# Decode attention and MLP on one core: K and V in tiles of four heads instead of two

## The chip, the cores and the metric

The kernel runs on one core of a Trainium2 chip. The metric is the device time of one execution in microseconds (us). Engines: PE (matrix products, with weight loads shown as PEld), DVE (vector), ACT (scalar), POOL, and SP, which here only issues DMAs. 16 DMA engines move data between HBM and SBUF.

## The reference, cut to what matters

One token, x of 576 numbers, goes through an attention block over a cached window and through an MLP; a gate mixes the two.

```python
W = 4096; Hq, Hkv, Dh = 32, 16, 128; D = 576; F = 4608
q = (x @ wq).reshape(1, 1, 32, 128)
k = repeat(k_cache[:, :, Sk - W:, :], 2); v = repeat(v_cache[:, :, Sk - W:, :], 2)   # Sk = 32768
p = softmax(einsum(q, k) * Dh ** -0.5)
a = einsum(p, v).reshape(1, 1, 4096) @ wo
b = gelu_tanh(x @ w1 + b1) @ w2 + b2
g = sigmoid(sum(x * gate_w))
out = g * a + (1 - g) * b
```

All tensors are bf16. K and V windows are 16.8 MB each, wq and wo 4.7 MB each, w1 and w2 5.3 MB each: 53.6 MB that are read once.

## The kernel before

All large loads are issued by SP, in program order. A K or V tile holds two heads: partition p holds 64 positions of one head, 16 KB (`load_kv`, L99). Six such buffers are used in turn by K, V and at the end w2 (`kv_pool`); three buffers hold wq, then w1, then wo (`w_pool`). A load into a buffer waits until its last reader is done, and what stands behind it in SP's queue waits with it.

The work is cut into 16 units (`NU`, half a tile each). For each unit h, `transposes` (L243) turns the keys with 32 matmuls against an identity, in eight groups of four; each group of 512 columns is copied out of PSUM, three by DVE (L257), five by ACT (L259). `scores` (L271) then multiplies q with the turned keys, two groups of four matmuls a unit. q lies in `qz` between zeros, so that each matmul puts its rows where they belong and adds zeros to the others. With two heads to a tile, turned keys of both heads alternate in the columns; a mask takes away those of the other head.

Four units make a batch of 128 rows by 512 columns. `softmax` (L287) runs in four steps: `row_max` (mask and maximum, DVE), `turn_max` (the maximum over rows, through PE), `spread` (the exponential on ACT), `put` (four PE transposes and eight DVE copies into `ez`, the form in which the weights stand for the next product). There are four batches. `values` (L346) multiplies ez with V, eight matmuls a unit, summed in `acc`; `heads_out` (L363) takes the heads from acc (four DVE operations on `a_s`) and turns them by one matmul.

The loop at L562 writes the order by hand: in loop h stand the transposes of unit h + 1, the scores of unit h, one step of the waiting softmax (`chain`), of heads_out (`tail`) or of the gelu (`mlp`), and the values of unit h - 6. w1's two halves are multiplied (`w1_mul`, 36 matmuls each) after loops 2 and 8; then `gelu` turns the 4608 numbers of h by 36 matmuls of 64 columns (L494). After the loop come the last softmax, the last values, wo's product (L684, 64 matmuls), w2's first three quarters in the same PSUM tile, `part_s` (L692), the last quarter of w2 into `y_ps` (L703), and the output.

Of the kernel before, what the change touches and what calls it, by code (L numbers as in the profile page):

```python
# [16 lines left out]
def kernel(  # L17
# [24 lines left out]
    NCK = W // (P // 2)  # L42
    NCH = NCK // 2
    NU = 2 * (Hkv // 2)
# [19 lines left out]
    HB = 4  # L64
    NB = Hkv // HB
    R = 2 * HB
    RP = R // 2
    BC = 4
    NBL = NCH // BC
    NGR = 2 * NBL // NQ  # L70
    MASK = -1.0e30


# [3 lines left out]
    kv_pool = ctx.enter_context(tc.tile_pool(name="kv_pool", bufs=6))  # L77
    w_pool = ctx.enter_context(tc.tile_pool(name="w_pool", bufs=3))
    const = ctx.enter_context(tc.tile_pool(name="const", bufs=1))
    kT_pool = ctx.enter_context(tc.tile_pool(name="kT_pool", bufs=2))  # L80
    small = ctx.enter_context(tc.tile_pool(name="small", bufs=2))
# [13 lines left out]
    OJ = 8  # L95
# [3 lines left out]
    def load_kv(cache, m, name):  # L99
        t = kv_pool.tile([P, NCK, Dh], BF16, name=name, tag="kv")  # L100

        nc.sync.dma_start(
            out=t[:],
            in_=cache[0, 2 * m : 2 * m + 2, Sk - W : Sk, :].rearrange(
                "e (p c) d -> p e (c d)", c=NCK
            ),
        )
        return t
# [46 lines left out]
    k_tiles[1] = load_k(1)  # L155

# [5 lines left out]
    qz = const.tile([P, Hkv // 2, 56], BF16, name="qz")  # L162
# [17 lines left out]
    for o in range(2):  # L180
# [22 lines left out]
    row_e = const.tile([P, 2], FP32, name="row_e")  # L203
    nc.vector.tensor_reduce(
        out=row_e[:], in_=ident_f[:].rearrange("p (a e q) -> p e a q", e=2, q=2), axis=AX.XY,
        op=ALU.add,
    )
    nc.vector.tensor_scalar(
        out=row_e[:], in0=row_e[:], scalar1=-MASK, scalar2=MASK, op0=ALU.mult, op1=ALU.add
    )  # L210
    mask = const.tile([P, BC * P], BF16, name="mask")
    for e in range(2):
        nc.vector.tensor_copy(
            out=mask[:, e::2], in_=row_e[:, e : e + 1].to_broadcast([P, BC * P // 2])
        )
# [15 lines left out]
    nc.gpsimd.memset(x2[:], 0.0)  # L231

# [10 lines left out]
    def transposes(h, i):  # L243
# [3 lines left out]
        for c in range(BC):  # L247
            nc.tensor.matmul(  # L248
                tp[:, c * P : (c + 1) * P],
                lhsT=k_tiles[h // 2][:, (h % 2) * NCH + i * BC + c, :],  # L250
                rhs=ident[:],
                start=True,
                stop=True,
            )
# [9 lines left out]

    ez = const.tile([P, 2, HB // 2, 2 * NBL, BC, R], BF16, name="ez")
    nc.gpsimd.memset(ez[:].rearrange("p a b c d e -> p (a b c d e)"), 0.0)
    b1_r = const.tile([P, 2, FB], BF16, name="b1_r")
    nc.gpsimd.memset(b1_r[:], 0.0)
    sums = const.tile([P, NB], FP32, name="sums")

    def scores(h, s):  # L271

        b, ul = h // HB, h % HB
        if ul == 0 and s == 0:
            s_tiles[b] = ps_s.tile([P, BC * P], FP32, name="s_ps", tag="s")
        lo = R * (NGR - 1 - 2 * (h % 2) - s)
        for t in range(NQ):
            i = 4 * s + t
            nc.tensor.matmul(  # L279
                s_tiles[b][32 * t : 32 * (t + 1), :],  # L280
                lhsT=qz[:, h // 2, lo : lo + 32],
                rhs=kT[h][:, i * BC * P : (i + 1) * BC * P],
                start=(ul == 0 and s == 0),
                stop=(ul == HB - 1 and s == 1),
            )

    def softmax(b):  # L287
# [3 lines left out]
        ms = small.tile([P, BC * P], FP32, name="ms", tag="ms")  # L291
        m8 = small.tile([1, R], FP32, name="m8", tag="m8")
        m_all = small.tile([1, P], FP32, name="m_all", tag="m_all")
        nb = small.tile([P, 1], FP32, name="nb", tag="nb")
        pr = small.tile([P, BC * P], BF16, name="pr", tag="pr")

        def row_max():
            nc.vector.tensor_tensor_reduce(
                out=ms[:], in0=s_ps[:], in1=mask[:], scale=1.0, scalar=-3.0e38,
                op0=ALU.add, op1=ALU.max, accum_out=mx[:],  # L300
            )

        def turn_max():
# [3 lines left out]
                out=m8[:], in_=mT[:].rearrange("o (s r) -> o r s", r=R), axis=AX.X, op=ALU.max  # L307
            )
            nc.vector.tensor_copy(
                out=m_all[:].rearrange("o (s r) -> o s r", r=R),  # L310
                in_=m8[:].rearrange("o (s r) -> o s r", s=1).to_broadcast([1, P // R, R]),
            )

        def spread():
# [6 lines left out]
                out=pr[:], in_=ms[:], func=ACT.Exp, bias=nb[:, 0:1], scale=SCALE,  # L321
                accum_out=sums[:, b : b + 1],
            )

        def put():
            pT = ps_m.tile([P, BC, P], BF16, name="pT", tag="m")
            for c in range(BC):
                nc.tensor.transpose(  # L328
                    out=pT[:, c, :], in_=pr[:, c * P : (c + 1) * P], identity=ident[:]
                )  # L330
            for m in range(HB // 2):
                for s in range(NGR):
                    nc.vector.tensor_copy(  # L333
                        out=ez[:, b % 2, m, NQ * s : NQ * (s + 1), :, RP * m : RP * (m + 1)],
                        in_=pT[:].rearrange("p c (t s r) -> p t c s r", t=NQ, r=R)[
                            :, :, :, s, RP * m : RP * (m + 1)
                        ],
                    )

        return [row_max, turn_max, spread, put]  # L340
# [5 lines left out]
    def values(h, i):  # L346

        b, ul = h // HB, h % HB
        if ul == 0 and i == 0:

            pool, tag = (ps_t, "tp") if b == NB - 1 else (ps_o, "o")
            acc[b] = pool.tile([P, BC, Dh], FP32, name="acc", tag=tag)
        ct = i % NQ
        n = (h % 2) * NBL + i
        nc.tensor.matmul(  # L355
            acc[b][32 * ct : 32 * ct + 4 * R, :, :],
            lhsT=ez[:, b % 2, ul // 2, n, :, :].rearrange("p c r -> p (c r)"),
            rhs=v_tiles[h // 2][:, n * BC : (n + 1) * BC, :],
            start=(ul == 0 and i < NQ),
            stop=(ul == HB - 1 and i >= NBL - NQ),  # L360
        )

    def heads_out(b):  # L363


        def take():
            nc.vector.tensor_scalar(
                out=a_s[:], in0=acc[b][:, 0, :], scalar1=m_c[:, 0:1], scalar2=None, op0=ALU.mult
            )
            for c in range(1, BC):  # L370
                nc.vector.scalar_tensor_tensor(  # L371
                    out=a_s[:], in0=acc[b][:, c, :], scalar=m_c[:, c : c + 1], in1=a_s[:],
# [3 lines left out]
        def turn_out():  # L376
            o_ps = ps_m.tile([P, R], FP32, name="o_ps", tag="m")
            nc.tensor.matmul(o_ps[:], lhsT=a_s[:], rhs=m_r[:], start=True, stop=True)  # L378
            nc.vector.tensor_copy(out=o_sb[:, b * R : (b + 1) * R], in_=o_ps[:])
# [34 lines left out]
    for h in range(2):  # L414
        for i in range(NBL):
            transposes(h, i)

# [14 lines left out]
    qT = ps_m.tile([P, QC // Dh, 2, NB], FP32, name="qT", tag="m")  # L432
# [10 lines left out]
    for m in range(HB // 2):  # L443
        lo = R * (NGR - 1) + RP * m
        nc.vector.tensor_copy(  # L445
            out=qz[:, m :: HB // 2, lo : lo + RP],
            in_=qT[:, :, m, :].rearrange("p i b -> p b i"),
# [29 lines left out]
    def gelu():  # L477
# [3 lines left out]
        h_r = const.tile([P, 2, FB], FP32, name="h_r")  # L481
        box = []

        def take():
            nc.vector.tensor_tensor(  # L485
                out=h_r[:], in0=h_box[0][:, :, 0:FB], in1=b1_r[:], op=ALU.add
            )
            box.append(ps_m.tile([P, RJ, NG], FP32, name="hT", tag="m"))

        def turn_h(j):  # L490

            rows = h_r[:].rearrange("p k n -> p (k n)")
            for e in range(2):
                nc.tensor.matmul(  # L494
                    box[0][64 * e : 64 * (e + 1), j, :],
                    lhsT=rows[:, j : j + RJ * 63 + 1 : RJ],
                    rhs=sel_f[:, e, :],
                    start=True,
                    stop=True,
                )  # L500

        def act():
            hacc = const.tile([P, NF], FP32, name="hacc")
            nc.vector.tensor_copy(out=hacc[:], in_=box[0][:].rearrange("p j g -> p (j g)"))
# [23 lines left out]
    def norm():  # L528

        sg = const.tile([P, NB, R], FP32, name="sg")  # L530
        nc.vector.tensor_tensor(
            out=sg[:],
            in0=sums[:].rearrange("p (b o) -> p b o", o=1).to_broadcast([P, NB, R]),
            in1=m_r[:].rearrange("p (o r) -> p o r", o=1).to_broadcast([P, NB, R]),
# [23 lines left out]
    W1_AT = {1: 0, 7: 1}  # L558
    LAG = HB + 2
    chain, tail, mlp = [], [], []  # L560
    w1_ready = None
    for h in range(NU):  # L562
        if 1 <= h < NU - 3 and h % 2 == 1:
            k_tiles[(h + 3) // 2] = load_k((h + 3) // 2)
        if h >= HB and h % 2 == 0:
            v_tiles[(h - HB) // 2] = load_v((h - HB) // 2)
        if h == 1:

            for o in range(2):
                nc.sync.dma_start(  # L570
                    out=b1_r[o : o + 32 * (NQ - 1) + 1 : 32],
                    in_=B_b1.rearrange("(o t k n) -> o t k n", o=2, t=NQ, k=2)[o],
                )
        w1_next = (W1_AT[h], w1_load(W1_AT[h])) if h in W1_AT else None
        for i in range(NBL):
            if 1 <= h < NU - 1:
                transposes(h + 1, i)

            at = (4, 6) if h % HB == 0 else (2, 5)
            if i in at:  # L580
                scores(h, at.index(i))
            if i in (0, 1, 3, 6) and chain:
# [3 lines left out]
            for f in (mlp[0:1], mlp[1:4], mlp[4:7], mlp[7:10], mlp[10:11])[i] if i < 5 else []:  # L586
                f()
            if h >= LAG and i % 4 == 3:
# [162 lines left out]
```

## Time and profile before

| | |
|---|---|
| runs | 134.14 us median of 3 (134.01 to 134.49) |
| profiled execution | span 132.4 us from the first to the last instruction |
| granted PE clock, mean | 0.853 |
| DMA | 53.79 MB in 4839 packets, mean 406 GB/s over the span |
| PE, PEld | 92.7 us busy (70%), 60.2 (45%) |
| DVE, ACT, POOL | 61.6 (47%), 49.3 (37%), 4.2 (3%) |
| transposes, 512 matmuls | 47.8 us, 247 ns each |
| copies of turned keys | ACT 80 of 586 ns, DVE 48 of 689 ns |
| exponential, 128x512 | 722 ns, four times |

The time of a run is that of the whole execution; the span is 1.7 us shorter than their median. Matmuls are pipelined, so a mean of 247 ns is no spacing: four of 128 columns follow each other in 0.22 us at full clock. DMA slices of the page give the mean busy share of the 16 engines in tenths.

### The profile page before, as it was taken

The page shows a single profiled execution, that of the slowest core. Times are in us where ns is not written, and L with a number is a line of the kernel's source. Part 1 is how long each engine was busy: PE and PEld are TensorE (multiplying, and loading weights), DVE is VectorE, ACT ScalarE, POOL GpSimd, SP SyncE. Part 2 cuts the span into 40 slices and gives each one's busy share as a digit, 9 for nine tenths or more (in the row PEclk, how much of TensorE's full clock was granted, in tenths as well). Part 3 has the DMA queues.
Part 4 walks back from the last instruction along what each step waited for, and adds up shares of the span by engine and source line. Part 5 has one row for each costly group of instructions (what it writes and reads, how often), then busy time and mean ns, then how long its engine had stood idle before and what let it go on. Part 6 is the DMA issues. An engine that isn't in the chain of part 4 may idle for free.

```text
span 132.4 us, 2667 instructions
## 1 busy us (share of the span) xinstructions
PE 92.7 (70%) x1127; PEld 60.2 (45%) x1127; DVE 61.6 (47%) x166; ACT 49.3 (37%) x93; POOL 4.2 (3%) x11
## 2 busy tenths in 40 slices
PE   0005996399099589995977999959988648377461
PEld 0005872266076466663546665645555224144230
DVE  4946452045104867457242576582665463530021
ACT  0301780067106587774532345745575200000001
POOL 8400000000000000000000000000000000000000
PEclk9999999769856999999599559995899965777975
DMA  4999999999999999999999999999999999999960
GB/s 104 446 434 442 434 423 416 445 435 439 416 421 436 426 441 413 436 447 418 424 421 436 421 436 426 436 436 411 445 421 441 400 432 426 433 431 411 425 265 5
DMA packets 4839, 53.79 MB, mean 406 GB/s; under 512 B 718, under 2 KB 860, under 8 KB 1500
## 3 DMA queue, kind: packets, MB, share of 16 engines
q1 hardware_dynamic: 4818, 53.62, 95.8%
q8 instruction: 9, 0.15, 0.4%
q14 instruction: 2, 0.02, 0.0%
q10 hardware_dynamic: 10, 0.00, 0.0%
HBM read 53.62 MB, written 0.00 MB: 405 GB/s over the span
## 4 chain that ended last, share of the span: by engine, by line
DMA 60%; PE 27%; DVE 7%; issue 2%; ACT 1%; SPq 1%; DVEq 0%; POOLq 0%; POOL 0%; ACTq 0%
DMA w_t<-in_B_w_dram 42%; DMA k_t<-in_A_k_cache_dram 15%; PE tp L248 12%; PE s_ps L279 4%; PE acc L355 4%; DMA b_r<-in_B_b_dram 3%; DVE kT L257 3%; PE hT L494 2%; DVE a_s L371 2%; PE y_ps L703 2%; PE h_ps L467 1%; ACT kT L259 1%; DVE part_s L692 1%; DVE h_r L485 1%; PE o_ps L378 0%
## 5 line engine op out<-in xcount | busy, mean ns | idle before, releaser
L259 ACT CAST kT<-tp 128x512 bf16<-128x512 f32 x80 | 44.3, 586 | 42.5 <-PE tp L248 42.1
L248 PE MATMUL tp<-ident,k_t 128*128 128x128 bf16 x512 | 47.8, 247 | 3.7 <-DMA k_t<-in_A_k_cache_dram 2.2
L257 DVE CAST kT<-tp 128x512 bf16<-128x512 f32 x48 | 32.9, 689 | 37.1 <-PE tp L248 33.4
L248 PEld LDWEIGHTS <-k_t 128*128 128x128 bf16 x512 | 37.4, 112 | 17.1 <-issue 13.5
L279 PE MATMUL s_ps<-kT,qz 128*32 128x512 bf16 x128 | 14.4, 442 | 0.3 <-DVE qz L445 0.3
L355 PE MATMUL acc<-v_t,ez 128*32 128x512 bf16 x128 | 13.3, 461 | 1.6 <-DVE a_s L371 1.3
L719 ACT CAST y<-y_ps 1x144 bf16<-1x144 f32 x2 | 0.5, 268 | 23.5 <-PE y_ps L703 23.5
L386 PE MATMUL x_ps<-x,dup 64*128 64x9 bf16 x1 | 0.2, 165 | 9.7 <-DMA x<-in_A_x_dram 9.7
L467 PE MATMUL h_ps<-w_t,x 128*32 128x288 bf16 x72 | 4.0, 365 | 3.7 <-DMA w_t<-in_B_w_dram 3.7
L355 PEld LDWEIGHTS <-ez 128*32 128x32 bf16 x128 | 3.7, 102 | 5.1 <-issue 2.9
L279 PEld LDWEIGHTS <-qz 128*32 128x32 bf16 x128 | 3.3, 95 | 4.2 <-issue 1.5
L692 DVE SCALAR_TENSOR_TENSOR part_s<-b_r,omg,part 128x576 f32<-128x576 bf16 x1 | 0.8, 812 | 9.5 <-PE part L684 9.5
L684 PE MATMUL part<-w_t,gt 128*1 128x288 bf16 x54 | 2.9, 285 | 3.1 <-DMA w_t<-in_B_w_dram 3.1
L467 PEld LDWEIGHTS <-x 128*32 128x32 bf16 x72 | 2.9, 118 | 4.6 <-issue 4.0
L333 DVE COPY ez<-pT 128x64 bf16<-128x64 bf16 x32 | 3.6, 181 | 2.3 <-PE pT L328 2.1
L684 PE MATMUL part<-wo_t,ow 128*1 128x288 bf16 x64 | 3.8, 427 | 1.0 <-DVE ow L662 1.0
L320 ACT ACTIVATE pr<-ms,nb 128x512 bf16<-128x512 f32 x4 | 2.9, 722 | 4.1 <-DVE nb L317 4.1
L371 DVE SCALAR_TENSOR_TENSOR a_s<-acc,m_c,a_s 128x128 f32<-128x128 f32 x12 | 4.2, 351 | 0.4
L161 DVE CAST ident_f<-ident 128x128 f32<-128x128 bf16 x1 | 3.0, 3000 | 1.8 <-POOL ident masks.py:199 1.8
L378 PE MATMUL o_ps<-m_r,a_s 128*128 128x8 f32 x8 | 1.7, 289 | 3.0 <-DVE a_s L371 3.0
L494 PE MATMUL hT<-sel_f,h_r 128*64 128x4 f32 x36 | 2.7, 264 | 1.4 <-DVE h_r L485 1.4
L378 PEld LDWEIGHTS o_ps<-m_r,a_s 128*128 128x128 f32 x8 | 1.4, 218 | 4.9 <-DVE a_s L371 2.5
(83 smaller groups left out, 50.1 us busy)
## 6 DMA issues: line engine op xcount, KB each, us to landing
k_t<-in_A_k_cache_dram SPq DMA_DIRECT2D x8, 2048.0 KB, 20.4
v_t<-in_A_v_cache_dram SPq DMA_DIRECT2D x8, 2048.0 KB, 23.5
w_t<-in_B_w_dram SPq DMA_DIRECT2D x2, 2592.0 KB
wo_t<-in_A_wo_dram SPq DMA_DIRECT2D x2, 2304.0 KB
w_t<-in_B_w_dram SPq DMA_DIRECT2D x2, 1296.0 KB, 21.1
wq_t<-in_A_wq_dram SPq DMA_DIRECT2D x1, 2304.0 KB
wq_t<-in_A_wq_dram SPq DMA_DIRECT2D x1, 1792.0 KB, 9.1
w_t<-in_B_w_dram SPq DMA_DIRECT2D x1, 864.0 KB, 23.2
```

What stands on the lines that cost most here:

```text
L161: nc.vector.tensor_copy(out=ident_f[:], in_=ident[:])
L248: nc.tensor.matmul(tp[:, c * P : (c + 1) * P], lhsT=k_tiles[h // 2][:, (h % 2) * NCH + i * BC + c, :], rhs=ident[:], start=True, stop=True,)
L257: nc.vector.tensor_copy(out=dst, in_=tp[:])
L259: nc.scalar.copy(out=dst, in_=tp[:])
L279: nc.tensor.matmul(s_tiles[b][32 * t : 32 * (t + 1), :], lhsT=qz[:, h // 2, lo : lo + 32], rhs=kT[h][:, i * BC * P : (i + 1) * BC * P], st ...
L333: nc.vector.tensor_copy(out=ez[:, b % 2, m, NQ * s : NQ * (s + 1), :, RP * m : RP * (m + 1)], in_=pT[:].rearrange("p c (t s r) -> p t c s ...
L355: nc.tensor.matmul(acc[b][32 * ct : 32 * ct + 4 * R, :, :], lhsT=ez[:, b % 2, ul // 2, n, :, :].rearrange("p c r -> p (c r)"), rhs=v_tiles ...
L371: nc.vector.scalar_tensor_tensor(out=a_s[:], in0=acc[b][:, c, :], scalar=m_c[:, c : c + 1], in1=a_s[:], op0=ALU.mult, op1=ALU.add,)
L378: nc.tensor.matmul(o_ps[:], lhsT=a_s[:], rhs=m_r[:], start=True, stop=True)
L467: nc.tensor.matmul(h_box[0][32 * t : 32 * (t + 1), k, 0:FB], lhsT=x2[:, m, :], rhs=w[:, off : off + FB], start=(m == 0), stop=(m == NM - 1),)
L494: nc.tensor.matmul(box[0][64 * e : 64 * (e + 1), j, :], lhsT=rows[:, j : j + RJ * 63 + 1 : RJ], rhs=sel_f[:, e, :], start=True, stop=True,)
L684: nc.tensor.matmul(part[32 * t : 32 * t + 1, k, 0:DB], lhsT=col, rhs=w[:, i * D + k * DB : i * D + (k + 1) * DB], start=(n == 0), stop=(n ...
```

## The change

K and V tiles hold four heads: a partition holds 128 positions of one head, 32 KB. There are four tiles each of K and V, three buffers instead of six, and two buffers instead of three for the other weights. A tile makes four units. The turned keys are permuted by `perm` instead of the identity, so that the columns of one head stand together, and each score matmul takes one head's columns (runs of 32, 128 apart): no mask. A batch has 128 rows again, but 8 units: two softmax batches instead of four. The exponential writes every number four times (once for each head place); `put` is four matmuls against `pick` and one DVE product with `own_r`, four times a batch. The loads' order and the places of values, w1_mul and gelu in the hand-written order are new. wo is read sixteen rows to a partition (18 KB in one piece). h is laid out twice over so that nine matmuls of 128 columns turn it; `half` picks the right copy. w2's first three quarters share one buffer.

```diff
-    NCK = W // (P // 2)
-    NCH = NCK // 2
-    NU = 2 * (Hkv // 2)
+    HT = 4
+    NT = Hkv // HT
+    PI = P // HT
+    NCK = W // PI
+    UT = 4
+    NCH = NCK // UT
+    NU = NT * UT
...
-    kv_pool = ctx.enter_context(tc.tile_pool(name="kv_pool", bufs=6))
-    w_pool = ctx.enter_context(tc.tile_pool(name="w_pool", bufs=3))
+    kv_pool = ctx.enter_context(tc.tile_pool(name="kv_pool", bufs=3))
+    w_pool = ctx.enter_context(tc.tile_pool(name="w_pool", bufs=2))
...
-            in_=cache[0, 2 * m : 2 * m + 2, Sk - W : Sk, :].rearrange(
+            in_=cache[0, HT * m : HT * (m + 1), Sk - W : Sk, :].rearrange(
                 "e (p c) d -> p e (c d)", c=NCK
...
-                rhs=ident[:],
+                rhs=perm[:],
...
+        kT_v = kT[h][:].rearrange("p (c g i) -> p c g i", g=HT, i=PI)
+        for g in range(HT):
             nc.tensor.matmul(
-                s_tiles[b][32 * t : 32 * (t + 1), :],
-                lhsT=qz[:, h // 2, lo : lo + 32],
-                rhs=kT[h][:, i * BC * P : (i + 1) * BC * P],
+                s_tiles[t // TB][32 * g : 32 * (g + 1), :, :],
+                lhsT=qz[:, HT * t + g, lo : lo + 32],
+                rhs=kT_v[:, s * CB : (s + 1) * CB, g, :],
...
-            nc.vector.tensor_tensor_reduce(
-                out=ms[:], in0=s_ps[:], in1=mask[:], scale=1.0, scalar=-3.0e38,
-                op0=ALU.add, op1=ALU.max, accum_out=mx[:],
+            nc.vector.tensor_copy(out=ms[:], in_=s_ps[:])
+            nc.vector.tensor_reduce(
+                out=mx[:], in_=ms[:].rearrange("p c i -> p (c i)"), axis=AX.X, op=ALU.max
             )
...
+                out=pr[:].rearrange("p c i g -> p (c i) g"),
+                in_=ms[:].rearrange("p c (i g) -> p (c i) g", g=1).to_broadcast(
+                    [P, CB * PI, HT]
+                ),
+                func=ACT.Exp, bias=nb[:, 0:1], scale=SCALE, accum_out=sums[:, b : b + 1],
...
+        def put(n):
+            pT = ps_m.tile([P, BC, TB * NBK, R], FP32, name="pT", tag="m")
             for c in range(BC):
+                nc.tensor.matmul(
+                    pT[:, c, :, :].rearrange("p x r -> p (x r)"),
+                    lhsT=pr[:, n * BC + c, :, :].rearrange("p i g -> p (i g)"),
+                    rhs=pick[:].rearrange("p x g q -> p (x g q)"),
...
+            nc.vector.tensor_tensor(
+                out=ez[:, :, :, n, :, :].rearrange("p t b c r -> p c (t b) r"),
+                in0=pT[:],
+                in1=own_r[:].rearrange("p (a b r) -> p a b r", a=1, b=1).to_broadcast(
...
+            for k in range(2):
+                nc.vector.tensor_tensor(
+                    out=h_r[:, :, k, :],
+                    in0=h_box[0][:, k : k + 1, 0:FB].to_broadcast([P, 2, FB]),
...
+            nc.tensor.matmul(
+                box[0][:, j, :, :].rearrange("p e g -> p (e g)"),
+                lhsT=rows[:, j : j + RJ * (P - 1) + 1 : RJ],
+                rhs=sel_f[:].rearrange("p e g -> p (e g)"),
...
+    w1_t = [w1_load(0)]
+    for h in range(UT - 1):
+        for s in range(2):
+            scores(h, s)
+
     chain, tail, mlp = [], [], []
+    for h in range(UT - 1, NU):
+        if h == 2 * UT - 1:
+            k_tiles[3] = load_k(3)
+            w1_t.append(w1_load(1))
+        if h == 3 * UT - 1:
+            v_tiles[1] = load_v(1)
         for i in range(NBL):
+            if h < NU - 1:
                 transposes(h + 1, i)
+            at = (4, 6) if h % (TB * UT) == 0 else (2, 5)
             if i in at:
                 scores(h, at.index(i))
+            if i in (0, 1, 3, 6, 7) and chain:
                 chain.pop(0)()
             if i in (0, 5) and tail:
                 tail.pop(0)()
+            if i > 1 and mlp:
+                for f in mlp[:2]:
+                    f()
+                mlp = mlp[2:]
+            if h in (10, 11) and i % 2 == 1:
+                for j in range(4):
+                    n = (h - 10) * 16 + (i - 1) * 2 + j
+                    values(n // NBL, n % NBL)
+        if h == 11:
+            tail = heads_out(0)
+            w1_mul(0, w1_t[0])
+        if h == 13:
+            w1_mul(1, w1_t[1])
+            mlp = gelu()
+        if h == TB * UT - 1:
+            chain = softmax(0)
+    v_tiles[2] = load_v(2)
+    v_tiles[3] = load_v(3)
...
     row_max()
+    unit(UT)
     turn_max()
+    unit(UT + 1)
     spread()
+    unit(UT + 2)
+    unit(UT + 3)
+    take, turn_out = heads_out(1)
     take()
+    for f in puts:
+        f()
     turn_out()
     norm()
     sums_start()
+    for t in range(2, NT):
+        for h in range(t * UT, (t + 1) * UT):
+            unit(h)
+        take, turn_out = heads_out(t)
+        take()
+        turn_out()
...
+    for o in range(NOG):
         t = w_pool.tile([P, WMAX], BF16, name="wo_t", tag="w")
+        nc.sync.dma_start(out=t[:, 0 : OJ * D], in_=wo_view[:, o, :])
```

V0 is loaded after the transposes of the first tile, which stand before the loop now for all four of its units.

## The prediction

> **What bounds the kernel now.** I read the slices of the page first, then the queues, then a table of stretches, then the end of the chain and the last 30 us of the matmul engine.
>
> ```profile
> PEclk9999999769856999999599559995899965777975
> DMA  4999999999999999999999999999999999999960
> GB/s 104 446 434 442 434 423 416 445 435 439 416 421 436 426 441 413 436 447 418 424 421 436 421 436 426 436 436 411 445 421 441 400 432 426 433 431 411 425 265 5
> ...
> q1 hardware_dynamic: 4818, 53.62, 95.8%
> ```
>
> All 16 DMA engines are busy from the second slice to the last but one: 53.62 MB at about 430 GB/s. There is no hole to fill, so only a faster stream, or a shorter end behind it, can help; any hole costs its full length. The stretches (columns: length, busy time and count of PE, PEld, DVE, ACT, POOL, granted clock, DMA share, GB/s):
>
> ```profile
> 39.00:59.00 20.00, 18.09 (x225) 12.35 (x223) 11.65 (x28) 13.81 (x26) 0.00 (x0) 0.92 1.01 431
> 66.00:104.00 38.00, 33.27 (x408) 21.48 (x410) 20.91 (x59) 18.09 (x34) 0.00 (x0) 0.86 1.01 429
> 106.00:114.00 8.00, 5.13 (x40) 2.19 (x40) 4.02 (x18) 0.07 (x1) 0.00 (x0) 0.57 1.02 431
> 72.91:79.74 6.83, 6.83 (x63) 4.33 (x60) 4.53 (x13) 2.85 (x6) 0.00 (x0) 0.50 1.00 425
> ```
>
> The first two carry K and V in 16-KB packets, the third w_o in 9-KB packets: 429 to 431 GB/s for either. And PE is busy 18 us in 20: it is a second resource that is nearly full, and after a pause it runs for a while at half clock (fourth row). The end:
>
> ```profile
> 110.48 2.75 PE L355 MATMUL acc<-v_t,ez 128*32 128x512 bf16 x24
> 114.85 0.39 PE L378 MATMUL o_ps<-m_r,a_s 128*128 128x8 f32 x2 [1.62 <-DVE a_s L371]
> 115.78 0.35 PE L652 MATMUL ow_ps<-ot,turn 128*128 128x32 bf16 x8 [0.54 <-DVE ot L646]
> 117.11 3.80 PE L684 MATMUL part<-wo_t,ow 128*1 128x288 bf16 x64 [0.97 <-DVE ow L662]
> 120.74 0.90 PE L684 MATMUL part<-w_t,gt 128*1 128x288 bf16 x18
> 122.98 0.90 PE L684 MATMUL part<-w_t,gt 128*1 128x288 bf16 x18 [1.35 <-DMA w_t<-in_B_w_dram]
> 124.78 0.53 PE L684 MATMUL part<-w_t,gt 128*1 128x288 bf16 x9 [0.90 <-DMA w_t<-in_B_w_dram]
> 126.17 0.54 PE L684 MATMUL part<-w_t,gt 128*1 128x288 bf16 x9 [0.86 <-DMA w_t<-in_B_w_dram]
> ```
>
> PE waits for w2 three times, 1.35 + 0.90 + 0.86 = 3.1 us. That is the whole slack of the compute chain against the stream: if w_o's product begins more than 3.1 us later than at 117.11, PE sets the end and no longer the DMA. Behind 126.17 stand part_s (0.82) and y_ps (2.00), then the output.
>
> ```profile
> 103.51 22.61 DMA w_t<-in_B_w_dram
> ...
> 127.61 2.00 PE y_ps L703 x43
> ```
>
> **The change, part by part.** (1) *Packets.* K and V, 33.55 MB, are 2,048 packets of 16 KB and become 1,024 of 32 KB. The packet records of this trace give 612.9 ns for one of 16,384 bytes, 772.0 for 20,736, 347.9 for 9,216: a line of 27.2 bytes per ns and 9 to 10.5 ns on top. If that top is paid per packet, 1,024 x 10 ns / 16 engines = 0.64 us are saved. The packets overlap a little, though (DMA share 1.01), and the stretches above show no dependence on size at all: lower bound 0. From 44.6 to 104.5 us the stream moves 25.7 MB, 429 GB/s, or 611 ns per 16-KB packet against 602 at 27.2 bytes per ns, which speaks for most of the gain being real: I take 0.45. w_o (512 packets of 9 KB become 256 of 18 KB): 256 x 6 to 9 ns / 16 = 0.1. Eight loads fewer save eight small completion writes of 9 ns: 0.07. Sum 0.6 us, bounds 0 and 0.9.
>
> The Trainium skill ("DMA: Bandwidth & Descriptors", section "Where 436 GB/s comes from") puts the fabric's ceiling at 435 GB/s; by it K and V could at best go from 78.2 us (at 429) to 77.1, a gain of 1.1 and no more.
>
> (2) *Order of loads and three buffers instead of six.* Each of the three 32-KB buffers is taken in turn: K0, K1, K2; then V0 when K0 is transposed, K3 when K1 is, V1 when K2 is, V2 when V0 is multiplied, V3 when K3 is transposed. A load whose buffer isn't free holds up all behind it in SP's queue: wo and w2. Times at which the stream needs each one, at 431 GB/s (a 4.19-MB tile 9.7 us, a half of w1 6.2, wq's 4.7 MB 11): x arrived behind K0 at 9.7 before, and K0 is 2.1 MB longer: 14.5. Then wq and K1 to 33.8, K2 43.5, V0 53.2, w1 59.4, K3 69.1, w1 75.3, V1 85.0, V2 94.7, V3 104.4.
>
> PE's side, from its timeline. First transposes 2.2 us behind x as before (9.70 to 11.88): 16.7. Four units at 3.5 (52 of 64 transposes took 5.67): 30.7; q and its turn 3.4 (19.20 to 22.64) and six groups of scores of 0.31: 36.0. A loop of 32 transposes and 8 scores takes 3.3 (first scores of one to the next at 49.70 and 52.91); with 8 values 3.6 (52.91 to 56.50). Loops 3 to 7: 52.5. Loops 8 and 9 hold the one softmax of 128 rows that runs under transposes. Before, such a loop took 7.3 (86.15 to 93.46), 3.7 over the plain one, part of it half clock. Now the maximum takes two DVE operations (0.69 for the copy; the reduce has no row of its size, 0.37 for 128 columns and 0.69 for a pass over 512, I take 0.6) for 0.68: +0.6. The exponential writes each number four times, 2,048 columns: 0.72 us for 512 and 0.24 for 36 make 1.02 ns each, so 2.3 us: +1.6. Four `put`s replace one, each with its 0.4 of matmuls and a product of 512 columns (0.7) in one PSUM buffer, so they go one by one, 1.1 each, partly under transposes: +3. So 2 x 3.3 + 3.7 + 5.2 = 15.5: 68.0. Loops 10 and 11 carry 16 values each: 4.1, so 72.1 and 76.2; K3 is there at 70. w1 1.4 (its 36 matmuls), loop 12 with the heads' turn on DVE 4.4, loop 13 3.3, w1 1.4: 86.7. Loop 14 has the gelu: 3.3, the wait for h_r of 1.4 as before (there are two DVE operations of 0.75 now, but three groups of transposes and one of scores run ahead of the wait), and nine turns of two matmuls: 36 matmuls took 2.5 (three times 12 in 0.8), so 18 take 1.3 to 2.5. Its last transpose: 86.7 + 3.3 + 1.4 + 1.9 = 93.3.
>
> So V1's buffer is free at 72 (needed at 75.3), V2's at 76 (85.0), V3's at 93.3. V3 must be issued some 1 us ahead (first load issued at 0.73, first packet at 1.77): at 93.7. No hole, by 0.4 us. That is close; the sum of twelve loops is not better than 2 us.
>
> (3) *The end.* Behind the last transposes: scores, gelu's DVE work and the maximum 3.9, turn and spread 1.4, exponential 2.5, four puts 4.6, o_ps and norm 1.2, then 32 values 2.7 to 3.7, `take` and turn 2.1, again 32 values 2.7 to 3.7, take to ow 4.8 (before: 113.29 to 117.11 = 3.8, with 8 more matmuls and two DVE operations of twice 256 columns). Sum 25.9 to 27.9 by the clock that the values get; I take 26.4, since the first 32 follow the puts and the second a pause of 2. So w_o begins at 119.7, 2.6 later than 117.11. The slack is 3.1, less the 0.6 that the stream gains: this chain comes out 0.1 late, level with the stream.
>
> (4) *The rest.* The mask goes, perm, pick, own, half and a turn of 2,048 columns come: some 2 us of DVE before 9 us, while it waits for x until 14.5; uncovered it would cost these 2 us. b1's two loads move to the front of SP's queue, behind K1; the first waits there for K0's landing, since it takes over that load's semaphore, and K2 behind it is issued at 15 to 16 us, while wq and K1 keep the engines busy until 33.8: nothing, and 18 us of cover. One point has no row: the scores now read kT in runs of 32 columns, 128 apart. Bounds: 0, or twice the 0.33 of a group, 32 x 0.33 = 10.6 us of PE. I take 0, since every operand with a step in the trace (h_r in steps of 9) ran at the pace of its shape. *Sum:* the profiled span 132.4 - 0.6 + 0.1 = 131.9; the median of the runs, 134.14, lies 1.7 above the span, and that stays: 133.6 us.
>
> **The rivals.** *B, the compute chain sets the end.* For it: the 0.1 us above, PE's bunching (idle until 16.7 instead of 11.9, all transposes in a row) and the half clock after each wait: the four puts leave PE idle for most of 5 us, and 6.8 us at half clock cost some 2 us of loops. Against it: fewer turns, three softmax chains less. Decided where w_o begins later than 119.6; at 1 to 3 us more the time is 134.5 to 136.6, say 135.3. *C, a hole in the stream before V3.* The same lateness, 2 us or more at unit 15, makes SP's queue wait, and wo and w2 behind it; decided at 93.7 us; with PE at 96 to 97 it is 136 to 137.5, and slower than before. *D, the packets bring nothing,* or four heads 8 MiB apart cost rate. The rows against it: two heads so far apart already run at 429 GB/s. Time 134.2; at 2% less rate for K and V 135.8. The Trainium skill ("DMA: Bandwidth & Descriptors", "Latency and other measured facts") has copies with row pitches of 4 and 8 MiB at half the rate; the trace, 429 GB/s with rows alternating between two heads, does not agree for this pattern.
>
> **How the numbers follow.** A measurement of this kernel tells 0.5%, 0.67 us, from no change: faster is below 133.47, slower above 134.81. The forecast A (stream-bound, 133.0 to 134.1) has 0.47, half of it below 133.47. B 0.30, of which 0.05 stay within the bound. C 0.14, all slower. D 0.09: 0.05 same, 0.04 slower. Faster 0.24, same 0.33, slower 0.43. The range 133.1 to 136.6 leaves out the best of A and the worst of B and C; A's own is 133.0 to 134.1.
>
> **What would show it.** Packet records of about 1,215 ns for 32 KB; 430 to 433 GB/s; no slice under 9 in the DMA row before the last two; V3 issued before 94; w_o's product at 119 to 121. Wrong if a DMA slice falls near 94 (C), if PE no longer waits for w2 (B), or if the scores take 0.5 us a group.

## The result and the profile after

| | before | after |
|---|---|---|
| runs, median (range) | 134.14 us (134.01 to 134.49) | 135.87 us (135.38 to 137.02) |
| ratio, 95% interval | | 1.0135 (1.0105 to 1.0166) |
| profiled execution, span | 132.4 us | 134.1 us |
| granted PE clock, mean | 0.853 | 0.866 |
| DMA packets, q1's share | 4839, 95.8% | 3431, 94.3% |

The changed kernel is slower, by 1.7 us in the span and in the medians. (Ratios here leave out disturbed runs, so a ratio can differ a little from the quotient of two medians.) The slices and the queue of the page of the changed kernel, the same rows as shown of before:

```profile
PEclk9999999999999999995999999965555558965797
DMA  4998999899998998999989999998998999999950
GB/s 115 511 450 350 432 450 489 371 425 472 459 410 376 469 452 355 458 446 469 415 380 458 467 420 401 445 449 362 322 459 357 394 418 440 427 426 413 423 201 6
...
q1 hardware_dynamic: 3410, 53.62, 94.3%
```

A slice is 3.35 us. Single 8s in the DMA row mean little: a round of sixteen 32-KB packets is 0.52 MB, and whether it ends just before or behind a slice's border moves that slice's GB/s. What counts is the queue's share, 1.5 points less of a longer span, and the 29th slice (93.9 to 97.2 us), the lowest in the middle of the row at 322 GB/s. Its digit in the DMA row is still a 9, because the slow packets in it count as busy time. It is the stretch behind the issue of V3. The tile's view and two stretches of the same profile (columns as before: length, busy time and count of five engines, clock, DMA share, GB/s):

```profile
L104 SPq DMA_DIRECT2D v_t<-in_A_v_cache_dram x4: 534/538/575, 30.1 to 93.3; - x4
```

```profile
66.00:92.00 26.00, 23.49 (x313) 16.30 (x310) 11.89 (x21) 13.35 (x24) 0.00 (x0) 0.92 1.00 427
93.00:98.00 5.00, 3.55 (x28) 0.67 (x26) 3.55 (x12) 0.82 (x2) 0.00 (x0) 0.50 0.84 308
```

V3, the last of the four V tiles, is issued at 93.3. Up to 92 the engines are full; from 93 to 98 they are at 0.84 and move 308 GB/s. What V3 waited for is PE's timeline (start, length, line, operation, count; in brackets the idle time before and what ended it). L539 are the nine turns of the gelu, two instructions each; L281 are transposes:

```profile
86.44 0.64 PE L539 MATMUL hT<-sel_f,h_r 128*128 128x8 f32 x2 [1.40 <-DVE h_r L528]
86.94 0.38 PE L281 MATMUL tp<-perm,k_t 128*128 128x128 bf16 x4
87.16 1.07 PE L539 MATMUL hT<-sel_f,h_r 128*128 128x8 f32 x4
88.09 0.59 PE L281 MATMUL tp<-perm,k_t 128*128 128x128 bf16 x4
...
91.78 1.04 PE L539 MATMUL hT<-sel_f,h_r 128*128 128x8 f32 x4
92.68 0.59 PE L281 MATMUL tp<-perm,k_t 128*128 128x128 bf16 x4
```

The last four transposes, behind the last turns, end at 93.27 and free K3's buffer; SP issues V3 0.03 us later. And the end of PE's timeline:

```profile
120.33 4.01 PE L734 MATMUL part<-wo_t,ow 128*1 128x288 bf16 x64 [1.50 <-DVE ow L712]
124.13 2.31 PE L734 MATMUL part<-w_t,gt 128*1 128x288 bf16 x36
126.67 0.53 PE L734 MATMUL part<-w_t,gt 128*1 128x288 bf16 x9 [0.24 <-DMA w_t<-in_B_w_dram]
128.08 0.54 PE L734 MATMUL part<-w_t,gt 128*1 128x288 bf16 x9 [0.88 <-DMA w_t<-in_B_w_dram]
129.53 0.43 PE L753 MATMUL y_ps<-part_s,row_f 128*1 128x144 f32 x8 [0.91 <-DVE part_s L742]
130.13 1.42 PE L753 MATMUL y_ps<-w_t,gt 128*1 128x144 bf16 x36 [0.18 <-DMA w_t<-in_B_w_dram]
```

w_o's product begins 3.2 us later than before (117.11), and of the 3.1 us that PE waited for w2 only 0.24 + 0.88 = 1.1 are left. Both tight places show at once: the stream lost time at 93, and the compute chain is nearly as late as the delayed stream.

### The profile page after: what moved, and what is told of

Read it like the earlier page. It is cut to its first block, busy times and chain, and to the rows that moved or that the text cites. A ratio compares the mean times of both kernels' runs of the same rounds, so it can differ in the third digit from the quotient of the medians.

```text
span 134.1 us, 2614 instructions
## 1 busy us (share of the span) xinstructions
PE 91.1 (68%) x1127; PEld 59.4 (44%) x1127; DVE 63.3 (47%) x138; ACT 50.3 (37%) x89; POOL 2.9 (2%) x10
## 2 busy tenths in 40 slices
DMA packets 3431, 53.79 MB, mean 401 GB/s; under 512 B 590, under 2 KB 732, under 8 KB 1372
## 3 DMA queue, kind: packets, MB, share of 16 engines
q1 hardware_dynamic: 3410, 53.62, 94.3%
## 4 chain that ended last, share of the span: by engine, by line
DMA 39%; PE 33%; DVE 15%; ACT 5%; issue 4%; SPq 1%; DVEq 0%; ACTq 0%
DMA k_t<-in_A_k_cache_dram 16%; PE tp L281 14%; DMA w_t<-in_B_w_dram 14%; DMA x<-in_A_x_dram 9%; PE acc L397 6%; ACT kT L292 5%; DVE kT L290 5%; PE hT L539 3%; PE s_ps L311 2%; DVE ez L373 2%; PE h_ps L509 2%; DVE a_s L413 2%; PE q_ps L465 2%; PE pT L366 1%; DVE h_r L528 1%
## 5 line engine op out<-in xcount | busy, mean ns | idle before, releaser
L281 PE MATMUL tp<-perm,k_t 128*128 128x128 bf16 x512 | 44.8, 234 | 4.3 <-DVE kT L290 2.1
L281 PEld LDWEIGHTS <-k_t 128*128 128x128 bf16 x512 | 35.4, 107 | 15.2 <-issue 12.7
L311 PE MATMUL s_ps<-kT,qz 128*32 128x512 bf16 x128 | 12.8, 415 | 0.4 <-DVE qz L487 0.3
L397 PE MATMUL acc<-v_t,ez 128*32 128x512 bf16 x128 | 12.7, 506 | 0.0
L366 PE MATMUL pT<-pick,pr 128*128 128x128 bf16 x32 | 4.1, 271 | 5.6 <-DVE ez L373 4.2
L373 DVE TENSOR_TENSOR ez<-pT,own_r 128x512 bf16<-128x512 f32 x8 | 5.5, 688 | 4.1 <-PE pT L366 4.1
L366 PEld LDWEIGHTS <-pr 128*128 128x128 bf16 x32 | 2.9, 121 | 7.7 <-issue 5.1
L539 PE MATMUL hT<-sel_f,h_r 128*128 128x8 f32 x18 | 4.9, 378 | 1.4 <-DVE h_r L528 1.4
L355 ACT ACTIVATE pr<-ms,nb 128x2048 bf16<-128x2048 f32 x2 | 4.0, 2002 | 4.9 <-DVE nb L352 4.9
L539 PEld LDWEIGHTS hT<-sel_f,h_r 128*128 128x128 f32 x18 | 4.7, 332 | 2.1 <-DVE h_r L528 1.7
```

Of the source, the lines that this page charges most:

```text
L281: nc.tensor.matmul(tp[:, c * P : (c + 1) * P], lhsT=k_tiles[h // UT][:, (h % UT) * NCH + i * BC + c, :], rhs=perm[:], start=True, stop=True,)
L311: nc.tensor.matmul(s_tiles[t // TB][32 * g : 32 * (g + 1), :, :], lhsT=qz[:, HT * t + g, lo : lo + 32], rhs=kT_v[:, s * CB : (s + 1) * CB, ...
L355: nc.scalar.activation(out=pr[:].rearrange("p c i g -> p (c i) g"), in_=ms[:].rearrange("p c (i g) -> p (c i) g", g=1).to_broadcast([P, CB ...
L366: nc.tensor.matmul(pT[:, c, :, :].rearrange("p x r -> p (x r)"), lhsT=pr[:, n * BC + c, :, :].rearrange("p i g -> p (i g)"), rhs=pick[:].r ...
L373: nc.vector.tensor_tensor(out=ez[:, :, :, n, :, :].rearrange("p t b c r -> p c (t b) r"), in0=pT[:], in1=own_r[:].rearrange("p (a b r) -> ...
L397: nc.tensor.matmul(acc[t][32 * ct : 32 * ct + BC * R, :, :], lhsT=ez[:, t % TB, n // NN, n % NN, :, :].rearrange("p c r -> p (c r)"), rhs= ...
```

## The experiments

Theory T (H in the expectations): the nine turns stand ahead of K3's last transposes, so V3 is issued about 1 us too late, and the hole in the stream is the loss. The rivals: the compute chain behind the last transposes sets the end (B), or the 32-KB packets are no gain, or are dearer (D, there S).

**e1, fill the hole with another load.** The first half of w_o, whose buffer is free, is loaded between V2 and V3; PE's work is unchanged.

```diff
...
     v_tiles[2] = load_v(2)
+    load_wo(0)
     v_tiles[3] = load_v(3)
+    load_wo(1)
...
```

> The changed kernel with the first half of wo loaded between V2 and V3, and the second behind V3, so that SP has a load to issue while V3 waits for K3's transposes. Theory H (the stream lost about 0.85 us in the hole at 93.5 to 95.8 us, and the rest of the 1.7 in the stream itself): the hole is filled, 134.9 us against 135.9 for the changed kernel, no DMA slice under 9 near 94. Rival B (the compute chain sets the end): last transposes at 93 and wo's product at 120 as before, so the time stays at 135.9. Rival S (all of the loss lies in the 32-KB packets): 135.9 as well.

Measured: 134.2 us (133.46 to 135.7), ratio 0.9986 (0.996 to 1.0013); V3 is issued at 93.29, as late as ever. Its stretch from 93 to 98 us, and the end of its PE timeline:

```profile
93.00:98.00 5.00, 3.55 (x28) 0.67 (x25) 3.53 (x12) 0.82 (x2) 0.00 (x0) 0.50 0.92 396
```

```profile
120.31 4.01 PE L738 MATMUL part<-wo_t,ow 128*1 128x288 bf16 x64 [1.50 <-DVE ow L716]
124.10 3.07 PE L738 MATMUL part<-w_t,gt 128*1 128x288 bf16 x54
128.08 0.43 PE L757 MATMUL y_ps<-part_s,row_f 128*1 128x144 f32 x8 [0.91 <-DVE part_s L746]
```

The engines are busy to within 0.02 us as in the changed kernel, and only the DMA differs: 396 GB/s instead of 308. The last packet of w2 ends 2.2 us earlier (at 128.64 instead of 130.86). Now PE goes through all 54 matmuls of w2 without a wait: with the hole filled, the compute chain sets the end. So the hole is the loss against the kernel before, and the chain is the next bound, right behind it. The theory expected 134.9, as it gave the hole little more than the engines' idle time; filling it brought 1.7 us.

**e2, take the turns out of the way.** The nine turns and the gelu move from the loop to behind the values of the third V tile; h_r is still made in the loop.

```diff
-            mlp = gelu()
+            mlp, late = gelu()
...
         take()
+        if t == 2:
+            for f in late:
+                f()
         turn_out()
```

> The changed kernel with the nine turns of h and the gelu behind them moved out of loop 14, to the pause of PE behind the values of tile 2. Last transposes of unit 15 at 87 to 89 us instead of 93.3, V3 issued then, no hole. Theory H: 134.9, as the stream alone sets the end. Rival B: wo's product begins 4 us earlier, 134.3 or less. Rival S: 135.9.

Measured: 133.62 us, ratio 0.9961 (0.9946 to 0.9976). V3 is issued at 87.14. The DMA row of its page, and the end of its PE timeline:

```profile
DMA  4989999998999899999999989999998999999970
```

```profile
117.12 3.57 PE L739 MATMUL part<-wo_t,ow 128*1 128x288 bf16 x64 [1.50 <-DVE ow L717]
120.52 0.90 PE L739 MATMUL part<-w_t,gt 128*1 128x288 bf16 x18
122.36 0.90 PE L739 MATMUL part<-w_t,gt 128*1 128x288 bf16 x18 [0.94 <-DMA w_t<-in_B_w_dram]
124.16 0.53 PE L739 MATMUL part<-w_t,gt 128*1 128x288 bf16 x9 [0.91 <-DMA w_t<-in_B_w_dram]
125.57 0.54 PE L739 MATMUL part<-w_t,gt 128*1 128x288 bf16 x9 [0.88 <-DMA w_t<-in_B_w_dram]
```

No hole, and w_o's product begins at 117.12, where it was before the change: PE again waits three times for w2. This is the time that the prediction gave to the change (133.6), and the version is faster than both kernels, by 0.4% than the one before. The time lies below the 134.9 that the theory expected and within B's "134.3 or less": the move takes away the hole and the lateness of the chain at once, so e2 alone can't tell the two apart. e1 can.

**e3, both of these.**

> Both moves together. Theory H: 134.9, no more than either alone, since there is only one hole. Rival B: 134.3 or less. If the two add up (134.0), each removes something else.

Measured: 133.61 us, ratio 0.996 (0.9945 to 0.9975). Nothing is added to e2, as expected, though at 133.6 and not at 134.9. e1 against e2 and e3, 0.3 us by the ratios and 0.6 by the medians, is what the late chain costs once the hole is gone; the intervals of e1 and e2 overlap, so the size is no more than an estimate.

**e4, the changed kernel with 16-KB packets:** each K and V tile loaded by two DMAs of half a tile.

> The changed kernel with each K and V tile of four heads loaded by two DMAs of 64 positions each, so that packets are 16 KB again; all else as in the changed kernel. Theory H: packets of twice the size save nothing, since the trace of the changed kernel has 1227.9 ns for 32 KB, which is 2.00 times 612.9; the hole stays; 135.5 to 135.9. Rival S (32-KB packets cost the stream its rate): 134.3 to 134.8. The forecast's step (32 KB save 0.45 us): 136.3.

Measured: 135.44 us, ratio 1.0082 (1.0054 to 1.011). The hole stays (V3 at 93.53), and PE runs through all 54 matmuls of w2 without a wait, since w_o's product comes at 122.69. With the hole and the late chain in it, the kernel doesn't show the packets' price; 16-KB packets didn't make it slower.

**e5, four of the nine turns behind the last transposes.**

```diff
-                for f in mlp[:2]:
+                k = {2: 2, 7: 99}.get(i, 1)
+                for f in mlp[:k]:
                     f()
-                mlp = mlp[2:]
+                mlp = mlp[k:]
```

> The changed kernel with four of the nine turns of h behind the last transposes of unit 15 instead of before them; no instruction more or less. Theory H (the hole before V3, with its slow restart, is the loss): last transposes at about 91.2 us instead of 93.3, V3's first packets at 92.5, before the first engines run dry at 93.5; no hole, and 134.0 to 134.3, as in the kernel with wo's first half before V3, where the compute chain is as late as here. Rival B (the chain behind the last transposes sets the end by itself): 135.9, since wo's product begins at 120.3 as before.

Measured: 135.87 us as the median of all twelve runs (134.08 to 137.25), ratio 1.0061 (1.0026 to 1.0095): a miss. In the profile V3 is issued at 92.26 and the engines lose only 0.12 us there, so the hole did close. But in this profile the turns delay the scores and the maximum of the last softmax, PE runs at half clock from 87.6 to 118.3, and w_o's product comes at 123.24, with no wait for w2 behind it: the chain sets the end. The profiled execution took 136.61 us, and the runs scatter too widely to say how much of the hole's gain the chain takes in the others; that stays open.

**e6, the nine turns undone:** the changed kernel with the 36 matmul instructions of 64 columns, the one DVE sum and the one DVE copy of before, at the same place.

```diff
...
+            for e in range(2):
+                nc.tensor.matmul(
+                    box[0][64 * e : 64 * (e + 1), j, :],
+                    lhsT=rows[:, j : j + RJ * 63 + 1 : RJ],
...
-            nc.tensor.matmul(
-                box[0][:, j, :, :].rearrange("p e g -> p (e g)"),
-                lhsT=rows[:, j : j + RJ * (P - 1) + 1 : RJ],
...
```

> The changed kernel with h turned by 36 matmuls of 64 columns and one DVE sum, as before the change. Nine turns of two matmuls took 4.9 us (18 of 378 ns by their starts), 36 took 2.7 in the kernel before, mostly at a higher clock. If the nine are no gain: the wait for h_r stays at 1.4, last transposes between 91 and 93.3, and the hole shrinks or stays: 134.2 to 135.9. If the nine are a gain: last transposes later than 93.3, and more than 135.9.

Measured: 134.5 us, ratio 0.9998 (0.9966 to 1.003). The same stretch of its PE timeline as shown of the changed kernel:

```profile
86.38 0.41 PE L536 MATMUL hT<-sel_f,h_r 128*64 128x4 f32 x4 [0.74 <-DVE h_r L527]
86.72 0.40 PE L281 MATMUL tp<-perm,k_t 128*128 128x128 bf16 x4
87.05 0.65 PE L536 MATMUL hT<-sel_f,h_r 128*64 128x4 f32 x8
...
90.11 0.65 PE L536 MATMUL hT<-sel_f,h_r 128*64 128x4 f32 x8
90.69 0.40 PE L281 MATMUL tp<-perm,k_t 128*128 128x128 bf16 x4
```

Twice as many instructions take 2.66 us (0.34 for the first four, 0.58 for each eight, from one start to the next) instead of 4.19 (0.50 and 0.93, 0.89, 0.97, 0.90 for each four). The half clock isn't what makes the wide turns dear: from one start to the next it is 0.24 us per instruction before 87.94, at full clock, and behind it, at half clock, and 0.24 in e2, where they run at full clock from 103.2 to 106.4. The loop from the first transpose of the last unit to its last, one line of the changed kernel and one of e6:

```profile
83.87:93.27 9.40, 8.00 (x64) 6.77 (x63) 3.77 (x7) 2.24 (x4) 0.00 (x0) 0.72 1.02 437
```

```profile
84.47:91.09 6.62, 5.88 (x82) 4.65 (x81) 2.89 (x6) 2.25 (x4) 0.00 (x0) 1.00 0.95 408
```

Of the 2.78 us between them the turns are 1.53, the second DVE sum 0.66 (waits of 1.40 and 0.74), and the remaining 0.6 lie in transposes and scores that ran at half clock in the changed kernel (clock 0.72) and not in e6 (1.00). V3 is issued at 91.12, and the engines lose 0.03 us. One part of the change, undone alone, gives its loss back.

**e7, a longer hole.** One extra matmul, whose result is unused, reads K3's buffer some 2 us behind the last transposes (at 95.88); V3 waits for it.

> The changed kernel with one more matmul that reads K3's buffer behind the values of unit 4, at about 95.4 us (its result is not used), so that V3 is issued 2.1 us later than in the changed kernel, at 95.5. Theory H: the hole grows by 2.1 us, and so does the time: 137.8 to 138.1. If the changed kernel's loss is set by the compute chain: 135.9 to 136.5, as PE itself loses nothing.

Measured: 138.65 us, ratio 1.0305 (1.0256 to 1.0354); V3 issued at 96.20. The DMA row of its page:

```profile
DMA  4998999999999999999999999995599899999960
```

An issue 2.90 us later makes the engines idle for 2.44 us more (3.29 instead of 0.85), the profiled span 2.3 us longer and the median 2.8 us; against e11, the changed kernel again, the ratios differ by 1.8 us. So most of the added lateness is paid. But the level is higher than expected: the medians lie 5.0 and 2.2 us above e2, and the spans 4.7 and 2.4, which is 1.4 to 1.7 us more than the idle time.

**e8, e3 with 16-KB packets:** the price of the packets where no hole hides it.

> The kernel with wo's first half before V3 and the late gelu, with each K and V tile loaded by two DMAs in 16-KB packets. There is no hole, so the stream alone sets the time. If the 32-KB packets are worth their price per packet (1213 ns against 2 x 611, 9 ns for each pair, 1024 pairs over 16 engines = 0.6 us, less what packets overlap): 134.0 to 134.2 against 133.6 with 32 KB. If they are worth nothing: 133.6.

Measured: 134.24 us, ratio 1.0001 (0.9974 to 1.0028), 0.63 us above e3. The packet records give 613.2 ns for 16 KB in e8 and 1,217.2 for 32 KB in e2: 1,024 times (1,226.4 - 1,217.2) / 16 = 0.59 us. D's first half falls: the 32-KB packets bring what their records say.

**e9, e2 with the 36 narrow turns.**

> The changed kernel with h turned by 36 matmuls of 64 columns again and with these turns and the gelu moved behind the values of tile 2. Both the hole and the lateness of the compute chain are gone; the stream in 32-KB packets sets the time: 133.5 to 133.7, as with the nine turns in the same place (133.6), and PE waits for w2 three times before the end. If the nine turns cost something besides their place: 133.3 or less.

Measured: 133.91 us, ratio 0.9991 (0.996 to 1.0022). w_o's product begins at 113.99, 3.1 us earlier than in e2, and it isn't faster: PE waits longer for w2 (1.60, 2.22, 0.87, 0.51). The time lies 0.2 us above the range expected. With the stream whole and the chain early enough, nothing is left to gain on PE.

**e10, before with the nine turns alone.** Six buffers, the old order, the wide turns and their two sums.

> The kernel before with h turned by nine matmuls of 128 columns, that part of the change alone. The turns take 4.5 to 5 us instead of 2.5 in loop 9, and h_r 0.7 more, so the loops behind are 2.5 to 3.5 us later. Six buffers: V4's buffer was free 7 us before the stream needed it, so no hole. wo's product at 119.6 to 120.6 instead of 117.1, against a slack of 3.1: 134.1 to 134.7. If the time stays at 134.1 to 134.3, the nine turns do harm only where a buffer waits behind them; if it is 135.5 or more, they are dear in themselves.

Measured: 134.14 us, ratio 1.0011 (0.998 to 1.0043). In the median the same dear turns cost nothing with six buffers. The loads' lead can be used up there too: in the profiled execution, the longest of the twelve (136.74 us), V4 is issued at 82.42 us instead of 77.47, the engines lose 0.28 us between 84 and 86 us, and w_o's product begins at 122.00, later than the 119.6 to 120.6 expected. How often that happens isn't shown.

**e11, the changed kernel again, unaltered.**

> The changed kernel itself, unaltered, timed over more rounds beside the next one, since its first four runs lie between 135.4 and 137.0. Theory H: V3 issued at 93 or later, the hole and the slow restart are there again, and the mean stays between 135.5 and 136.2.

Measured: 136.31 us, a little above the range expected, ratio 1.0169 (1.0148 to 1.019). V3 is issued at 93.37, and the engines lose 1.05 us; w_o's product begins at 122.08, later than in the first profile, because the second tile's values after the last softmax ran at half clock (3.60 us instead of 1.91). There PE runs through w2 without a wait: on this run hole and chain both reach the end.

**e12, e2 with w_o in eight rows per partition** (9-KB packets again).

> The changed kernel with the late gelu (133.6) and with wo at eight rows to a partition again, 9-KB packets. By the forecast's price 256 packets more of 6 to 9 ns over 16 engines cost 0.1 us: 133.6 to 133.8. If the sixteen rows mattered for the compute chain (ow's two DVE operations are half as long with eight), 133.6 as well, since the stream sets the end there.

Measured: 134.12 us, ratio 1.0001 (0.9979 to 1.0023), 0.5 us above e2, where 0.1 was expected. Two packets of 9 KB take 694.0 ns, one of 18 KB 686.0 in e2: 256 x 8 / 16 = 0.13 us. The sign is as forecast, the size a miss. In the profiled execution (134.81 us) the last packet of w2 ends at 129.30 instead of 128.32, and 0.7 of that 1.0 us is idle time of engines that finish before the last one (behind 125 us, 1.33 us per engine instead of 0.61); why they finish further apart stays open.

## Why the prediction failed

It forecast the stream as the bound, without a hole, at 133.6. The mechanism that it called C (a hole in the stream before V3), with a chance of 0.14, decided instead.

**Packets (1): right.** 32-KB packets took 1,217 ns on average up to the hole (about 1,215 forecast); the gain taken was 0.45 us, within bounds of 0 and 0.9, and e8 against e3 measured 0.63. The sign that was to show it in GB/s couldn't: 427 from 66 to 92 us, but a single round of 32-KB packets is 20 GB/s in 26 us.

**V3's issue (2): the step that failed** is "V3 must be issued some 1 us ahead ... at 93.7. No hole, by 0.4 us". The last transposes were forecast for 93.3 and ended at 93.27, and V3 went out at 93.30. Yet the first DMA engines were dry at 93.5. Two sizes were off. The first packet came 1.3 us after the issue, at 94.6, not 1.0. And the 94.7 at which V2 was to end was taken for all 16 engines, but they end apart: the first at 93.5, the last V2 packet at 95.3. The dry engines didn't take over packets of the others: six packets of V2 started only between 93.79 and 94.05, each where another packet ended, while other engines already stood dry. So V3 was due at 93.5 - 1.3 = 92.2. The runs bear it out: issued at 91.12 (e6) 0.03 us were lost, at 92.26 (e5) 0.12, at 93.30 0.85, at 96.20 (e7) 3.29.

**The turns: mis-sized, and covered up by another error.** Nine turns of two instructions were given 1.3 to 2.5 us by the narrow ones' price; they took 4.19. The wait for h_r was 1.40 as forecast, though e6 shows that the second sum is half of it. The last loop took 9.40 us, not 6.6. It began at 83.87 and not at 86.7, since the loops before it were shorter than their terms (the two with the softmax took 13.6 us, not 15.5), and the two errors of 2.8 us cancelled: that the last transposes ended at 93.27, as forecast, was luck. With 1.9 us for the turns, all else as it ran, V3 would have gone out at 91.0, and there would have been no hole: e6 is that case, at 91.12.

**The price of C: too low.** C said 136 to 137.5 for PE at 96 to 97; e7, at 96.20, took 138.65. Part of this is the due time, 92.2 and not 93.7. The rest can be read from the packets: in the changed kernel the last packet of w2 ends at 130.86, 2.22 us later than in e1. Of these, 0.85 are idle engines in the hole. The slow first packets behind it are 0.67: the last eighth of the 32-KB packets took 1,302 ns on average instead of 1,217, and 128 packets x 84 ns / 16 = 0.67. w_o's packets add 0.08 (689 ns instead of 686). And 0.58 are idle engines at the very end, which finish further apart than in e1: behind 125 us, 1.44 us per engine up to the last packet, instead of 0.86. That they do so because they restarted apart is likely, but not shown. The prediction gave a hole its length and had no term for the last three.

**The end (3): right to 0.6 us.** w_o's product was forecast for 119.7, and the chain "level with the stream"; it began at 120.33 (122.08 in e11). Rival B is there too, but not first: once the hole is filled it costs some 0.3 to 0.6 us (e1 against e2), and in the profile of e5 it sets the end. The two rivals were priced as alternatives, but the same late turns feed both.

**D and the rest (4): right.** The scores over runs of 32 columns keep the plain ones' pace, 0.33 us a group at full clock (e6, 88.87 to 89.20), and the new constants at the start left no hole. Four heads 8 MiB apart ran at 27 bytes per ns and engine (32,768 / 1,217); the half rate that the Trainium skill gives for copies between HBM tensors whose rows lie 4 or 8 MiB apart ("DMA: Bandwidth & Descriptors", section "Latency and other measured facts") doesn't show here either, where only the heads lie so far apart and the 32 rows of one head follow each other.

## What to carry to other kernels

Fewer buffers turn work on another engine into the stream's business: look for what stands ahead of the last reader of each buffer, and ask for a margin of 1 to 2 us, since here the DMA engines ended a transfer 1.8 us apart and the first packet came 1.3 us behind the issue. Half as many instructions needn't take half the time (here 4.19 us instead of 2.66); price a reshaped matmul by a row of its own weight shape, and put work that nothing waits for (here the gelu, needed at the very end) behind the work that frees buffers. When two tight margins hang on the same late step, fixing one shows the other, so undo each alone and both together.

## What the runs showed of the hardware that was not expected

**Wide fp32 turns are dearer than twice as many narrow ones.** The views of the tile hT (engine, count, shortest, median and longest in ns), the changed kernel and then e6:

```profile
L539 PEld LDWEIGHTS hT<-sel_f,h_r x18: 312/336/338, 86.4 to 92.4; 128*128 128x128 f32 x18
L539 PE MATMUL hT<-sel_f,h_r x18: 329/384/404, 86.4 to 92.4; 128*128 128x8 f32 x18
```

```profile
L536 PEld LDWEIGHTS hT<-sel_f,h_r x36: 194/217/219, 86.4 to 90.5; 128*64 128x64 f32 x36
L536 PE MATMUL hT<-sel_f,h_r x36: 260/262/283, 86.4 to 90.5; 128*64 128x4 f32 x36
```

A weight load of 128 columns takes 336 ns, one of 64 columns 217. The wide turns follow each other at about 0.47 us a turn (4.19 / 9), the narrow ones, which write two halves of the array's columns, at 0.29 (0.58 / 2) for a turn of four instructions. Both overlap, since the wide instructions start 0.24 us apart, less than one weight load; but the narrow ones start in pairs, 0.01 us apart, one pair every 0.12 us. So the narrow ones overlap far more; that the halves of the array are the cause is only argued.

**A hole in the stream costs more than its idle time.** In the first round behind the hole of the changed kernel, ten of the sixteen 32-KB packets take 1.8 to 2.4 us instead of 1.2, and the engines end the whole stream further apart. The stream ends 2.2 us later than in e1 for 0.85 us of idle time in the hole, and 4.2 us later (132.87) for 3.29 us in e7.

**Half clock lasts in steps.** In the changed kernel the granted clock falls at 87.94 and comes back at 111.84: 23.90 us, which is 7.0 times 3.413. The Trainium skill ("TensorE: Matmul & The Clock Gate", section "What's actually happening") has a free-running window of 3,413 ns, and the length agrees; it also says that one busy window is enough to come back, and there the trace doesn't agree, since PE was busy 3.41 of 3.41 us from 87.94 to 91.35 and stayed at half clock for six windows more. The full clock came back behind another window that was busy throughout:

```profile
87.94:91.35 3.41, 3.41 (x22) 2.78 (x22) 0.12 (x1) 1.17 (x2) 0.00 (x0) 0.50 0.93 404
108.43:111.84 3.41, 3.41 (x32) 0.95 (x24) 0.84 (x2) 0.00 (x0) 0.00 (x0) 0.50 1.01 432
111.84:115.25 3.41, 1.79 (x34) 1.05 (x34) 1.57 (x5) 0.00 (x0) 0.00 (x0) 1.00 1.01 432
```

Why the first of the two didn't bring it back isn't shown.
